# One product of each Winograd layer computed by seven products of quarters, with sums left running in PSUM

## The chip, the cores and the metric

The kernel runs on one core of one Trainium2 chip. Its time is the device time of one execution, in microseconds (us). Engines are named as in the profile: PE (TensorE matmul), PEld (its weight load), DVE (VectorE), ACT (ScalarE), POOL (GpSimd), SP (SyncE, which here only issues DMAs).

## The reference: what is computed

```python
# threshold attention: q, k, v of 8 batches x 8 heads x 576 rows x 64
scores = q @ k.T / 8
scores = where(scores >= max(scores) - tau, scores, -1e9)
attn   = softmax(scores)                   # per row
x      = (attn @ v) laid out as 4608 rows x 512
# hash routing: each row goes to one of 8 experts
expert = token_ids * 2654435761 % 8
for e in range(8):
    h = relu(x[expert == e] @ w1[e])       # 512 -> 1024
    out[expert == e] = h @ w2[e]           # 1024 -> 512
```

Everything is float32. A float32 matmul appears in the trace as two records of a matmul and two of a weight load.

## The kernel before, in words

The first part, up to about 477 us, is attention; the change does not touch it. Towards its end the routing tables are made, the first two experts' weights are loaded, and the first layer of the first expert is computed piece by piece (`early_h`, `late_h`, L633 to L666). `late_h` takes its last PSUM tiles from two pools in turn: `ps_sc` for fo 2 and 4, `ps_m` for fo 0, 1, 3 and 5.

The second part treats the experts one after the other, ordered by size. An expert has room for 544 (the first), 576 (the next four) or 600 (the last three) rows, which stand in the free dimension, cut in two halves of 272, 288 or 300 (240 in the second layer of the last expert, whose remaining 120 rows are done by `last_tile`). So a layer is out = W^T x with W cut into 2 x 2 blocks a11 to a22 and x into b11 to b22. Both layers use the Winograd form of Strassen's scheme: seven block products instead of eight, on four sums of each operand. `left` and `right` give the sums of the weights and of the inputs:

```python
return [sub(s3, a11, a21), add(s1, a21, a22), sub(s2, s1, a11), sub(s4, a12, s2)]
return [sub(t3, b22, b12), sub(b12, b12, b11), sub(t2, b22, b12), sub(t4, b21, t2)]
```

`seven` runs the products. Layer 1 calls it twice (groups g = 0 and 1, 256 of the 512 columns of a weight block each), each for two column blocks of 128; layer 2 calls it once with twice the inner length. In records: 8 a product in layer 1, 16 in layer 2, 112 a layer in both. A product goes into a PSUM tile of two banks; `bank2` takes them in turn from the pools `ps_sc` and `ps_m`, two tiles in each, four in all. ACT copies the first product out (`p1`), and DVE adds every other product to what is needed: c11 = p1 + a12 b21, u2 = p1 + s2 t2, u3 = u2 + s3 t3, c21 = u3 + a22 t4, u4 = u2 + s1 t1, c22 = u3 + s1 t1, c12 = u4 + s4 b22. In layer 1 ACT then applies Relu in place.

The order of the work around it is written out by hand. `seven` calls `after(step)` at six points, and `side1` and `side2` put there what other engines are to do meanwhile: the sums of the second layer's weights (`w2_work`), of h (`h_work`), of the next expert's weights and inputs (`x_work`), the transposes of the next expert's gathered rows (`turns`: five `squares` on DVE, then `move`, 16 DMAs on SP's queue that fill `xT`), the output transposes `put_squares(e, 0)` and `(e, 1)` on DVE, followed by some nine or ten row scatters each on POOL's queue, the row gathers `fetch(e + 2)` on POOL's queue, and the weight loads on SP's queue. Each engine works through its own list in this order and waits where data or a buffer is not there.

The second-layer weights of all experts but the last are read "dealt": the columns of one 128-wide stationary operand are every fourth word of the tile (every second word of the sums' tile).

Of the kernel before, what the change touches and what calls it, by code (L numbers as in the profile page):

```python
# [9 lines left out]
FP32 = mybir.dt.float32  # L10
# [10 lines left out]
def kernel(  # L21
# [17 lines left out]
    P = 128  # L39
# [787 lines left out]
    with tc.tile_pool(name="m_x", bufs=1) as m_x, \  # L827
         tc.tile_pool(name="m_o", bufs=3) as m_o, \
# [9 lines left out]
        o_end = m_x.tile([P, DIN], FP32, name="o_end")  # L838
# [4 lines left out]
        w2_s = m_s.tile([P, 3, FH, D2], FP32, name="w2_s")  # L843
        h_s = m_s.tile([P, 3, FH, CH], FP32, name="h_s")
        halves = [m_s.tile([P, 2, CH], FP32, name=n) for n in ("p1", "u2", "u3", "u4")]
# [3 lines left out]
        turn = [0]  # L849

        def bank2():
            turn[0] ^= 1
            if turn[0]:
                return ps_sc.tile([P, 2, 512], FP32, name="sc")
            return ps_m.tile([P, 2, 512], FP32, name="bank2")
# [31 lines left out]
        def w2_sums(e):  # L887
            t = triple(w2_s, 0, FH)
            return t if e == E - 1 else [dealt(x, C2) for x in t]
# [19 lines left out]
        def sums_w2(e):  # L909
            s1 = None  # L910
            if e == E - 1:
                spare = w_pool.tile([P, CO, F], FP32, name="w1_sb")
                s1 = w_tiles["s1"] = spare[:, :, 0:D2]
            return left(*w2_blocks(e, w_tiles[e, 2]), w2_sums(e), s1)
# [11 lines left out]
        def seven(a, a_s, b, b_s, m0, outs, relu, after):  # L926

            (a11, a12, s1, a22), (s2, s3, s4) = a, a_s
            (b11, t1, b21, b22), (t2, t3, t4) = b, b_s
            c11, c12, c21, c22 = outs  # L930
            n_k, width, dealt_out = a11.shape[1], b11.shape[2], len(a11.shape) == 4
            p1, u2, u3, u4 = (t[:, :, 0:width] for t in halves)

            def product(x, y):
                ps = bank2()
                for i in range(2):
                    c0 = m0 + P * i
                    for c in range(n_k):
                        lhsT = (x[:, c, :, i] if dealt_out else
                                x[:, c, c0:c0 + P])  # L940
                        nc.tensor.matmul(ps[:, i, 0:width], lhsT=lhsT, rhs=y[:, c],  # L941
                                         start=c == 0, stop=c == n_k - 1)
                return ps[:, :, 0:width]

            def out(c, ps, u, step):
                add(c, ps, u)()
                if relu:
# [249 lines left out]
```

## Time and profile before

| | |
|---|---|
| three runs, us | 944.19, 938.54, 937.22 (median 938.54) |
| the profiled execution's own time | 931.3 us |
| its span, first to last instruction | 929.7 us |
| granted TensorE clock | 0.996 |
| PE, DVE, ACT, POOL busy, us | 909.8, 757.5, 457.3, 403.7 |
| first record of the first expert's layer 2 | 501.02 us |
| last matmul group begins | 920.41 us |

A row of the order in time gives start and duration in us, engine, line, operation, output and inputs by tile name, shapes and the number of merged records. Names lose their numbers: `bank` is a tile of `ps_m`, `sc` one of `ps_sc`, `w_s` and `w_sb` are weight sums and weights, `h_s` and `x_s` sums of inputs. A matmul's end is modelled and overlaps the next one's start, so the cost of a product is read from start to start. A row of waits tells who waited for whom, in total, how often, and the longest.

### The profile page before, as it was taken

What the parts mean: (1) busy time and instruction counts of PE and PEld (TensorE: products, weight loads), DVE (VectorE), ACT (ScalarE), POOL (GpSimd) and SP (SyncE); (2) the same over time, 40 slices, a digit from 0 to 9 for tenths busy, and PEclk for the clock granted to TensorE, in tenths of its full rate; (3) what the DMA queues carried; (4) which work ended last, traced back from release to release, by engine and by line L of the source; (5) the groups of instructions that cost most, each with busy time, mean ns of one, the idle gap of its engine ahead of it and who ended that gap; (6) DMA issues with size and microseconds to landing.
All of it is one profiled execution on the core that took longest, in us unless ns stands there. A gap on an engine that the chain in (4) does not pass through costs nothing.

```text
span 929.7 us, 20725 instructions
## 1 busy us (share of the span) xinstructions
PE 909.8 (98%) x7495; PEld 662.0 (71%) x7495; DVE 757.5 (81%) x1654; ACT 457.3 (49%) x741; POOL 403.7 (43%) x528
## 2 busy tenths in 40 slices
PE   7999999999999999999999999999999999999996
PEld 4666666656666566665678888788887978878785
DVE  7999999999999999999955776767668676777551
ACT  6888888888888898888812010110201021020110
POOL 4232432456666623455423370724527073440702
PEclk9999999999999999999999999999999999999999
DMA  7354463554545668743101745364372536412101
GB/s 175 92 148 118 109 152 93 136 131 103 123 105 153 159 165 214 216 107 88 30 25 51 237 131 158 133 173 141 95 223 75 164 133 165 157 34 50 48 3 55
DMA packets 114775, 113.11 MB, mean 122 GB/s; under 512 B 32475, under 2 KB 89315, under 8 KB 114672
## 3 DMA queue, kind: packets, MB, share of 16 engines
q1 hardware_dynamic: 105168, 92.64, 37.0%
q0 software_dynamic: 9072, 18.91, 7.0%
q8 instruction: 61, 1.00, 0.4%
q14 instruction: 42, 0.34, 0.1%
q10 hardware_dynamic: 432, 0.21, 0.1%
HBM read 81.99 MB, written 21.44 MB: 111 GB/s over the span
## 4 chain that ended last, share of the span: by engine, by line
PE 65%; issue 21%; POOL 7%; DVE 3%; ACT 2%; DMA 1%; another core or an unknown queue 1%; POOLq 0%; SPq 0%; DVEq 0%; ACTq 0%
PE av L313 18%; PE sc L235 15%; PE tr L282 11%; PE sc L941 9%; PE bank L941 8%; POOL out_dram L1036 6%; PE sc L640 2%; PE av L282 1%; POOL xg L119 1%; ACT w L260 1%; DVE ns L246 1%; DVE w L271 1%; ACT wT_b L303 1%; ACT wT_a L303 0%
## 5 line engine op out<-in xcount | busy, mean ns | idle before, releaser
L260 ACT ACTIVATE w<-ns,nmx 128x576 f32<-128x576 f32 x288 | 220.5, 777 | 28.8 <-DVE ns L246 27.8
L271 DVE SCALAR_TENSOR_TENSOR w<-ns,thr,w 128x576 f32<-128x576 f32 x288 | 225.8, 816 | 0.0
L1036 POOL DMA_INDIRECT out_dram<-o_q,qidx x127 | 138.1, 1087 | 191.7 <-DVE o_q L1028 153.1
L246 DVE TENSOR_SCALAR_CACHE_REDUCE ns<-sc 128x576 f32<-128x576 f32 x288 | 205.6, 747 | 8.1 <-PE sc L235 7.4
L253 POOL TENSOR_SCALAR thr<-nmx,drop 128x2 f32<-128x2 f32 (+1 forms) x160 | 104.4, 653 | 187.3 <-DVE ns L246 177.6
L235 PE MATMUL sc<-k_sb,q 64*128 64x288 f32 (+1 forms) x1280 | 179.2, 423 | 1.0 <-DVE drop L704 0.7
L282 PEld LDWEIGHTS tr<-ident,w 64*128 64x128 f32 x2624 | 106.0, 138 | 95.4 <-ACT wT_b L303 32.4
L282 PE MATMUL tr<-ident,w 64*128 64x64 f32 x2624 | 139.5, 231 | 6.0 <-ACT wT_b L303 2.6
L948 ACT ACTIVATE h<-h 128x576 f32<-128x576 f32 (+1 forms) x56 | 38.7, 693 | 164.8 <-DVE h L861 126.1
L235 PEld LDWEIGHTS sc<-k_sb,q 64*128 64x128 f32 (+1 forms) x1280 | 93.0, 177 | 23.2 <-DVE ns L246 9.4
L313 PE MATMUL av<-wT_a,v 128*64 128x320 f32 (+1 forms) x704 | 100.6, 418 | 0.2
L303 ACT COPY wT_a<-tr 128x512 f32<-128x512 f32 (+1 forms) x128 | 81.7, 638 | 20.7 <-PE tr L282 20.2
L303 ACT COPY wT_b<-tr 128x512 f32<-128x512 f32 (+1 forms) x128 | 81.4, 636 | 17.1 <-PE tr L282 11.2
L313 PE MATMUL av<-wT_b,v 128*64 128x256 f32 x640 | 83.2, 389 | 0.0
L313 PEld LDWEIGHTS av<-wT_a,v 128*64 128x64 f32 x704 | 43.8, 137 | 29.3 <-DVE xm L352 0.7
L951 ACT COPY p<-bank 128x576 f32<-128x576 f32 (+2 forms) x11 | 7.0, 633 | 99.5 <-PE bank L941 72.5
L313 PEld LDWEIGHTS av<-wT_b,v 128*64 128x64 f32 x640 | 40.2, 136 | 18.8 <-issue 0.7
L542 POOL DMA_INDIRECT slot_scratch<-tok,slot_i x36 | 45.0, 1251 | 9.4 <-issue 7.6
L941 PE MATMUL bank<-h,w_sb 128*128 128x288 f32 (+3 forms) x192 | 48.1, 404 | 0.0
L941 PE MATMUL sc<-h,w_sb 128*128 128x288 f32 (+3 forms) x192 | 47.7, 401 | 0.0
L941 PEld LDWEIGHTS bank<-h,w_sb 128*128 128x128 f32 x192 | 46.6, 300 | 0.5
L941 PEld LDWEIGHTS sc<-h,w_sb 128*128 128x128 f32 x192 | 45.9, 289 | 0.6
(197 smaller groups left out, 1303.7 us busy)
## 6 DMA issues: line engine op xcount, KB each, us to landing
w_sb<-in_moe_w_dram SPq DMA_DIRECT2D x16, 2048.0 KB
q<-in_q_dram SPq DMA_DIRECT2D x62, 288.0 KB
v<-in_v_dram SPq DMA_DIRECT2D x32, 256.0 KB
x_scratch<-xm SPq DMA_DIRECT2D x32, 256.0 KB
xT<-xq SPq DMA_DIRECT2D x84, 80.0 KB
k_sb<-in_k_dram SPq DMA_DIRECT2D x31, 144.0 KB
k_sb<-in_k_dram SPq DMA_DIRECT2D x32, 112.0 KB
x_scratch<-xg SPq DMA_DIRECT2D x9, 256.0 KB
```

The lines of the kernel that those rows point to most:

```text
L235: nc.tensor.matmul(sc[out_rows, i, 0:S2], lhsT=q_sb[rows, h, q0:q1], rhs=k_sb[rows, h], start=True, stop=True)
L246: nc.vector.tensor_scalar(out=ns[:].rearrange("p (i s) -> p i s", i=2), in0=sc[:, :, 0:S2], scalar1=-1.0, scalar2=None, op0=ALU.mult, op1= ...
L253: nc.gpsimd.tensor_scalar(out=thr[:, 0:j + 1], in0=stats[n][0][:, 0:j + 1], scalar1=drop[:], scalar2=None, op0=ALU.add)
L260: nc.scalar.activation(w, nss[n, j][:], AF.Exp, bias=stats[n][0][:, j:j + 1], scale=-1.0)
L271: nc.vector.scalar_tensor_tensor(out=w, in0=nss.pop((n, j))[:], scalar=stats[n][1][:, j:j + 1], in1=w, op0=ALU.is_le, op1=ALU.mult, accum_ ...
L282: nc.tensor.transpose(dst[:, r, 64 * c:64 * c + 64], src[rows, c0:c0 + P], ident[rows, rows])
L303: nc.scalar.copy(dst, tr[:, :, 0:64 * n_c].rearrange("p r (c q) -> p r c q", c=n_c))
L313: nc.tensor.matmul(av[64 * j:64 * j + 64, g, c0:c1], lhsT=v_sb[:, c, 64 * j:64 * j + 64], rhs=wT[g][:, i, c0:c1], start=(c == 0), stop=stop)
L542: nc.gpsimd.indirect_dma_start(out=slot_dram[c % 2][:, :], out_offset=bass.IndirectOffsetOnAxis(ap=slot_i[:, c:c + 1], axis=0), in_=tok[:, ...
L941: nc.tensor.matmul(ps[:, i, 0:width], lhsT=lhsT, rhs=y[:, c], start=c == 0, stop=c == n_k - 1)
L948: nc.scalar.activation(c, c, AF.Relu)
L1036: inst = nc.gpsimd.indirect_dma_start(out=rows[:, :], out_offset=bass.IndirectOffsetOnAxis(ap=idx, axis=0), in_=o_sb, in_offset=None, boun ...
```

## The change

Three things are changed in the experts' part.

First, one of the seven products of each layer of experts 1 to 7, a12 b21, is itself computed by seven products of its quarters (class `Quarters`), again in Winograd's form. In layer 1 it covers both groups at once: its four results are written to c11's place in h, and each group's p1 is added to them there. Its operand sums are new: four of the weights (`inner_w`, into `wi_s`) and four of the inputs (`inner_b`, into `bi_s`), each a quarter of a block. For layer 2 of experts 1 to 6, ACT first copies the block a12 into contiguous quarters (`copy_quarters`, into `w2_q`). The sum s4 is then written over a12 (over a spare tile for the last expert), and `w2_s` shrinks to two blocks.

Second, sums run on in PSUM. u2 is formed by adding s2 t2 onto p1's bank, u3 by adding s3 t3 onto u2's, c21 by adding a22 t4 onto u3's; c12 is s4 b22 added onto s1 t1. ACT copies a bank out at each stage that is needed later (`p1`, `u2`, `mid`), and Relu of c21 reads PSUM. DVE is left with the sums for c11, c12 and c22. Four fixed tiles (`banks`) take the place of the alternation.

Third, expert 0's second layer, which keeps a whole a12 b21, begins in `banks[3]`, uses `banks[2]` and `banks[0]`, and has its products in another order (first, a12 b21, s2 t2, s1 t1, s3 t3, s4 b22, a22 t4). The side work is dealt out anew over eleven points in layer 1 and five in layer 2. The pool `m_o` and `o_end` go; `xg_bufs` take their place in the last outputs.

```diff
-        w2_s = m_s.tile([P, 3, FH, D2], FP32, name="w2_s")
+        w2_s = m_s.tile([P, 2, FH, D2], FP32, name="w2_s")
+        w2_q = m_s.tile([P, 4, 2, P], FP32, name="w2_q")
...
+        def late_tile(fo):
+            if fo in (2, 4):
                 return ps_sc.tile([P, 2, 512], FP32, name="sc")
             return ps_m.tile([P, 2, 512], FP32, name="bank2")
...
+        def products(ps, x, y, start, mid=None):
+            for i, lhsTs in enumerate(x):
+                for c, lhsT in enumerate(lhsTs):
+                    nc.tensor.matmul(ps[:, i], lhsT=lhsT, rhs=y[:, c], start=start and c == 0,
+                                     stop=c == len(lhsTs) - 1, skip_group_check=not start)
+                if i == 0 and mid:
+                    mid()
...
+        class Seven:
...
+            def first(self):
+                products(self.x, self.a[0], self.b[0], True)
+            def keep_p1(self):
+                nc.scalar.copy(self.p1, self.x)
+            def second(self, y):
+                y = y[:, :, 0:self.x.shape[2]]
+                products(y, self.a[1], self.b[2], True)
+                self.out(self.outs[0], y, self.p1)
+            def u2_sum(self):
+                products(self.x, self.a[4], self.b[4], False)
+                nc.scalar.copy(self.u2, self.x)
+            def s1_t1(self, keep):
+                products(self.z, self.a[2], self.b[1], True)
+                if keep:
+                    nc.scalar.copy(self.mid, self.z)
+            def u3_sum(self, keep):
+                products(self.x, self.a[5], self.b[5], False)
+                if keep:
+                    nc.scalar.copy(self.mid, self.x)
+            def c21(self):
+                products(self.x, self.a[3], self.b[6], False)
...
+            def c12(self, mid=None):
+                products(self.z, self.a[6], self.b[3], False, mid)
+                self.out(self.outs[1], self.z, self.u2)
...
+        class Quarters:
...
+            def p1_p2(self):
+                products(self.x, self.a[0], self.b[0], True)
+                nc.scalar.copy(self.p1, self.x)
+                products(self.y, self.a[1], self.b[2], True)
+            def c11(self):
+                add(self.outs[0], self.y, self.p1)()
+            def p5_u2(self):
+                products(self.z, self.a[2], self.b[1], True)
+                nc.scalar.copy(self.p5, self.z)
+                products(self.x, self.a[4], self.b[4], False)
+                nc.scalar.copy(self.u2, self.x)
+            def c12_c22(self):
+                products(self.z, self.a[6], self.b[3], False)
+                add(self.outs[1], self.z, self.u2)()
+                products(self.x, self.a[5], self.b[5], False)
+                add(self.outs[3], self.x, self.p5)()
+            def c21(self):
+                products(self.x, self.a[3], self.b[6], False)
+                nc.scalar.copy(self.outs[2], self.x)
...
         def layer1(e, side):
...
+            q = quarters_of(e, 1, *banks[1:])
+            g0, g1 = group(0, banks[0], banks[2]), group(1, banks[1], banks[3])
+            g0.first()
+            g0.keep_p1()
+            side(0)
+            q.p1_p2()
+            q.c11()
+            g0.u2_sum()
+            side(1)
+            q.p5_u2()
+            g0.s1_t1(True)
+            side(2)
+            q.c12_c22()
+            side(3)
+            g0.u3_sum(False)
+            q.c21()
+            g0.c22(g0.x)
+            side(4)
+            g0.c12()
+            g0.c11(g0.p1)
+            g1.first()
+            g0.relus()
+            side(5)
+            g1.c11(g1.x)
+            g1.relus()
+            g0.c21()
...
         def layer2(e, side):
...
+            o = Seven(a, w2_sums(e), h_blocks(0, FH, half), triple(h_s, 0, FH, half), 0, outs,
+                      False, *((banks[0], banks[1]) if e else (banks[3], banks[2])))
+            o.first()
+            o.keep_p1()
+            if e == 0:
+                o.second(banks[0])
+                run(w2_first)
+                side(0)
+                o.u2_sum()
...
+            q = quarters_of(e, 2, *(banks[i][:, 0:1] for i in (2, 3, 3)))
+            q.p1_p2()
+            q.c11()
+            run(inner_b(second_blocks(e, 2)[1]), 4)
+            o.u2_sum()
+            q.p5_u2()
+            side(0)
+            o.u3_sum(True)
...
         with tc.manual_schedule():
-            run(sums_w2(0), 4)
+            w2_first = sums_w2(0)
+            run(w2_first, 3)
...
+                    def side1(step):
+                        if step == 1 and e == 1:
+                            put_squares(0, 0)
+                        if step == (0 if e > 1 else 2):
+                            put_squares(e - 1, 1)
+                        if step == 2 and more:
+                            copy_quarters(e)
+                        run(w2_work, (0, 1, 2, 0, 3, 1, 1, 0, 0, 0, 0)[step])
+                        run(h_work, 2 if step in (8, 9) else 0)
+                        run(turns, (0, 0, 0, 0, 0, 0, 1, 2, 1, 1, 1)[step])
...
+                    run(x_work, ((1, 2, 3, 10, 0) if e else (2, 2, 0, 4, 8))[step])
...
-                    if more and step == 3:
+                    if more and e and step == 4:
                         put_squares(e, 0)
```

## The prediction

> **What bounds the kernel now.** I read the busy table first, then the expert stage alone (from about 501 us to the end): its stretches by layer, PE's own waits, and the order of products in time. All times here are microseconds of the profiled execution unless marked ns.
>
> The busy table of the page:
>
> ```profile
> PE 909.8 (98%) x7495; PEld 662.0 (71%) x7495; DVE 757.5 (81%) x1654; ACT 457.3 (49%) x741; POOL 403.7 (43%) x528
> ```
>
> PE never rests for long. The next view cuts experts 1 to 3 into layers (columns: stretch, its length, busy us of PE, weight loads, DVE, ACT, POOL, then clock and DMA share):
>
> ```profile
> 527.00:554.10 27.10, 27.10 (x113) 21.28 (x112) 24.37 (x31) 5.27 (x8) 20.08 (x19) 1.00 0.50 183
> 554.10:583.30 29.20, 27.58 (x114) 24.91 (x114) 19.17 (x22) 1.90 (x3) 5.91 (x7) 1.00 0.61 171
> 583.30:610.50 27.20, 27.20 (x114) 21.37 (x113) 20.65 (x26) 5.28 (x8) 20.72 (x20) 1.00 0.36 123
> 610.50:637.60 27.10, 27.10 (x113) 24.84 (x113) 19.45 (x23) 1.90 (x3) 2.87 (x3) 1.00 0.59 162
> ```
>
> The reader is to see that PE fills a layer from end to end, that DVE is at 70 to 90% of a layer and ACT at under 20%. All the time PE loses to others from 490 us on stands in PE's waits (line waited for: total, times, longest):
>
> ```profile
> PE bank L941 <- DVE h_s L858: 1.9, 2, 1.6
> PE sc L941 <- ACT p L951: 0.6, 1, 0.6
> PE bank L941 <- ACT p L951: 0.5, 1, 0.5
> PE bank L941 <- DVE h L861: 0.2, 1, 0.2
> PE sc L941 <- DVE h L861: 0.2, 1, 0.2
> ```
>
> That is 3.4 us in seven experts. So the stage is a stream of matmuls, and a change is worth what it takes out of that stream, minus the holes it makes. The price of one matmul comes from the order in time (start, duration, group, number of records; a float32 matmul shows as two records, each with its own weight load):
>
> ```profile
> 501.02 3.90 PE L941 MATMUL sc<-h,w_sb 128*128 128x272 f32 x16
> 504.76 3.90 PE L941 MATMUL bank<-h,w_sb 128*128 128x272 f32 x16
> 508.49 3.83 PE L941 MATMUL sc<-h_s,w_s 128*128 128x272 f32 x16
> 512.16 3.83 PE L941 MATMUL bank<-h_s,w_s 128*128 128x272 f32 x16
> ...
> 532.80 2.10 PE L941 MATMUL sc<-x_s,w_s 128*128 128x288 f32 x8
> 534.74 2.10 PE L941 MATMUL bank<-x_s,w_sb 128*128 128x288 f32 x8
> ...
> 920.41 1.91 PE L990 MATMUL sc<-w_sb,h 128*120 128x128 f32 x16
> ```
>
> Starts give the cost. 288 columns: 1.94/8 = 242.5 ns a record; 272 columns: 3.67/16 = 229.4 ns; both are columns x 0.833 ns + 2.5 ns. With weights read from the dealt (every fourth word) second-layer tile the 272 case takes 3.74/16 = 233.8 ns: there the weight load sets the pace, and at 288 it hides. Products of expert 5 to 7 (300 columns) start 2.02 apart: 252.5 ns. The last row, 128 columns against 120 weight columns, is (1.91 - 0.273)/15 = 109 ns a record with its last duration of 273 ns taken off: the same formula, so short matmuls keep the rate.
>
> **What the Trainium skill says.** "TensorE: Matmul & The Clock Gate", Back-to-back issue gap, says that in a stream of weight loads and matmuls both set the spacing, so that short matmuls fall behind the streaming rate; its section on LDWEIGHTS prices a load at columns / 1.2 GHz, an estimate of 107 ns for 128. The trace agrees that a load hides behind 288 columns, and its 109 ns row shows no extra at 128. "PSUM — Partial Sum Buffer", PSUM bank collisions raise a hardware error, says two engines must not touch a bank at once. So a product that adds onto a bank must wait until the copy out of it is done. The trace has such a hand-over: an ACT copy from 826.13 for 0.66, PE at 826.85, 0.06 later. Nothing before shows a PE that writes again onto a bank just read, which is the new thing here.
>
> **The change, part by part.**
>
> *Products.* In each of 14 layers (both of experts 1 to 7) the product a12 b21, 8 matmuls of half width (16 records; in layer 1 over both groups), becomes 14 matmuls of quarter width (28 records). For 288 columns: before 112 x 0.2425 = 27.16; after 96 x 0.2425 + 28 x (144 x 0.833 + 2.5 = 122.5 ns) = 23.28 + 3.43 = 26.71. Gain 0.45, eight layers: 3.6. For 300 columns: 28.28 against 24.24 + 28 x 0.1275 = 27.81; gain 0.47, five layers: 2.35. The last layer (240 columns, 202.5 ns; quarter of 120, taken at the measured 109) gains 22.68 - 19.44 - 3.05 = 0.2. Sum **6.1 us**, all on the path. The unknown is 28 short records with full 128-column weights: from below the formula's 122.5 ns, from above the 190 ns that one contiguous 128-column weight load lasts in the group rows, if loads didn't overlap each other. I take 122.5, because the 109 ns row has loads of 183 ns that do overlap. The dealt weights would cost 234 ns, but the change copies them to w2_q first.
>
> *DVE.* Each big set loses the adds for u2, u3, u4 and c21: 4 x 0.755 (576 elements), three sets an expert, 9.1 us. Added: six quarter adds and sixteen small sums. The slope between 576 elements (755 ns) and 1024 (1219) is 1.04 ns, so 288 costs 0.46, 256 0.42, 144 0.31: 3 x 0.46 + 3 x 0.31 + 8 x 0.42 + 4 x 0.31 + 4 x 0.46 = 8.8. DVE stays where it was, with 10 to 30% free; nothing lands on the path by volume, only by order.
>
> *ACT.* Copies of u2, mid and c21 (0.63 each, 0.69 with Relu replaced), four quarter copies (0.63 less 288 x 0.833 = 0.39) per layer and the weight copy (1024 elements, about 1.05): some 8 us an expert, on an engine with 7 busy of 54. Hidden by volume.
>
> *New waits of PE on ACT.* In each layer a set's first product is copied out and then added onto. ACT starts 0.24 after the product's end (585.23 to 585.47), takes 0.63, and PE resumes 0.06 later: 0.93. Between lie two quarter products, 8 x 122.5 ns = 0.98. Covered by 0.05; at 300 columns 0.96 against 1.02. The same margin stands before u3 in layer 2: three tight places an expert, 21 in all. The other re-used banks have a big product (1.94 or 3.88) in between. If that cover is gone each place costs up to 0.93. I take 0.
>
> *Expert 0's second layer.* It now begins in banks[3], the second of ps_m, whose last tenant is late_h's fo 5. DVE reads that one from 501.22 for 0.72; the first product started at 501.02 in the other pool. It must now wait to 502.0: **+1.0**. s4 moves into the dealt a12: 16 x 4.4 ns = +0.1. DVE's turns of x come behind the second product's add and s4, at about 511.6 instead of 509.4. SP then issues 16 moves of 0.6 us; they landed 12.3 us after the last turn (512.47 to 524.76), now near 527.0, against expert 1's first product near 528.0: hidden by 1 us. But the x sums (4 x 0.76) and the inner sums (4 x 0.31) wait for them until 531.2, and then DVE owes in layer 1 of expert 1: q.c11, put_squares(0,0) 1.9, a w2 sum 1.2, put_squares(0,1) 2.1, two sums 2.4, two quarter adds 0.8; it ends near 540.0. PE wants bank 1 for the quarter's c21 at 538.8: **+1.3**. Later experts have put_squares(e,0) a layer earlier and land with 0.6 us or more to spare, by the same ledger. POOL gets the output scatters a few us later; it is busy 26 of the 56 us of a layer pair (20.08 + 5.91). SP's queue: moves one step later in layer 1, needed 16 us into layer 2, landing about 9 us in.
>
> *What stays.* Four DVE waits of 10.0 us in all, and ACT waits of 1.4 and 2.8, are put down to "remote", no engine or queue of the program. They cause most of the 3.4 us above. The change doesn't touch their cause, so I keep 3.4, with 0 and 7 as ends. The tail after the last matmul (922.3 to the end) has the same steps.
>
> Sum: -6.1 + 1.0 + 0.1 + 1.3 = **-3.7**. The profiled execution took 931.3 (span 929.7 and 1.6 around it); it becomes 927.6. The median shown is 938.54, 7.2 above that execution, and I carry the difference over: **934.8**, 0.4% less.
>
> **Rivals.**
>
> *Slower: the banks' turn-round.* The mechanism: PE adds onto a bank that ACT or DVE has just read, at about eight places an expert (g0's u2, the quarter's c21, g1's u2, u3, c21; in layer 2 u2, u3, the quarter's c21), 56 in all. If queueing of copies and adds behind other work costs 0.3 each, that is 16.8: 938.5 - 3.7 + 16.8 = 951.6. It decides from (9.4 + 3.7)/56 = 0.23 us a place. For it: margins of 0.05 to 0.6 us, and in-order engines. Against: ACT is nearly idle, and DVE's waits are mostly for PE, not PE's for it.
>
> *Slower: weight loads.* At 190 ns the short records cost 392 x 67.5 ns = 26.5: 961. It passes +1% from 122.5 + 13.1/392 = 156 ns. Against: the 109 ns row.
>
> *Faster: the holes close.* If the 3.4 goes too and neither new hole of expert 0 and 1 appears: -9.5, 929.0, just over 1%. For it: four bank pairs instead of two in turn. Against: nothing removes the remote waits.
>
> *The change does not do what it says*: the banks tie products so that PE idles what it saves. That is the turn-round at 0.1 us a place: -3.7 + 5.6, 940.4, no change.
>
> **How the numbers follow.** Forecast 0.62, spread 931 to 939 by the ends of the remote waits and of the tight places; no gain (940.4) 0.07; turn-round 0.15; weight loads 0.06; faster 0.10. The range 929 to 946 leaves out the weight loads, the upper half of the turn-round and the faster end. A measurement of this kernel tells about 1%, 9.4 us, from no change. Faster by over 1%: 0.08 (part of the last case); slower by over 1%: 0.20; within: 0.72.
>
> **What would show it.** Products: 28 records of 144 columns a layer, 122.5 ns apart; layers of 26.7 where they were 27.2. PE's waits: about 1.0 before expert 0's first product, on DVE, and about 1.3 in expert 1 before the quarter's c21; under 0.1 at the copies. DVE busy about equal, ACT up by some 50 us. I am wrong if the short records stand at 150 ns or more, if PE's waits on ACT sum to over 5 us, or if DVE's sums of x come late in later experts.

## The result: 8.8 per cent slower, all of it in layer 1 of experts 1 to 7

The changed kernel takes 1021.88 us (median; 1011.1 to 1025.93), the kernel before, beside it on the same chip, 937.88: a ratio of the means of **1.0877** (95% interval 1.076 to 1.0993; of the medians it is 1.0896). The profiled execution took 1025.6 with a span of 1024.0, against 931.3 and 929.7.

The busy table and the 40 slices (each digit a tenth of a slice; PEclk is TensorE's granted clock) of the page after:

```profile
PE 928.9 (91%) x7663; PEld 680.8 (66%) x7663; DVE 756.0 (74%) x1720; ACT 513.5 (50%) x848; POOL 397.7 (39%) x528
...
PE   8999999999999999999996897985969969879697
...
PEclk9999999999999999999999897997979979979899
```

PE is no longer full from slice 22 on, and from slice 26 on its clock drops in six slices in which it rests or has just rested. The stretches of experts 1 and 2, layer 1 and layer 2 each (stretch, length, busy us of PE, weight loads, DVE, ACT, POOL, then clock, DMA share and GB/s):

```profile
528.10:571.30 43.20, 29.01 (x125) 22.44 (x124) 26.29 (x38) 11.85 (x18) 23.55 (x22) 0.88 0.54 175
571.30:598.40 27.10, 27.10 (x126) 25.43 (x126) 16.80 (x28) 4.12 (x9) 0.00 (x0) 1.00 0.22 78
598.40:639.50 41.10, 31.87 (x126) 24.64 (x125) 21.68 (x30) 11.17 (x17) 23.59 (x23) 0.83 0.39 119
639.50:666.50 27.00, 27.00 (x126) 25.33 (x126) 18.51 (x30) 4.13 (x9) 0.00 (x0) 1.00 0.35 106
```

Layer 2 takes 27.0 (26.7 reckoned); layer 1, 27.2 before, takes 43 and 41 here and 39 to 45 over the seven experts. POOL's column tells what lies beside the long layers and not beside the short ones: the row scatters, 17 or 18 of them, with five gathers of rows. PE's waits from 470 us on (line waited for: total, times, longest), 3.4 us before:

```profile
PE bank L939 <- DVE h L866: 36.0, 8, 10.5
PE bank L939 <- issue: 24.4, 4, 8.5
PE bank L939 <- ACT u L981: 14.3, 1, 14.3
PE bank L939 <- ACT h L1042: 4.2, 2, 2.1
```

Expert 2's layer 1 in order of time shows what such a wait is made of (start, duration, what ran, idle time before it and what ended that); PE's rows first, then DVE's, ACT's, and POOL's first and last scatter:

```profile
606.64 0.65 PE L939 MATMUL bank<-bi_s,wi_s 128*128 128x144 f32 x4
607.13 2.10 PE L939 MATMUL sc<-x_s,w_s 128*128 128x288 f32 x8
611.57 1.21 PE L939 MATMUL bank<-bi_s,w_sb 128*128 128x144 f32 x4 [2.33 <-DVE h L866]
612.57 3.38 PE L939 MATMUL sc<-xT,w_s 128*128 128x288 f32 x8
622.85 4.21 PE L939 MATMUL bank<-xT,w_sb 128*128 128x288 f32 x8 [6.90 <-issue]
...
611.06 0.46 DVE L866 TENSOR_TENSOR h<-bank,q_p 128x288 f32<-128x288 f32 x1 [3.06 <-remote]
617.54 0.76 DVE L866 TENSOR_TENSOR h<-sc,u 128x576 f32<-128x576 f32 x1 [6.03 <-PE sc L939]
...
622.39 0.40 ACT L1042 COPY h<-bank 128x288 f32<-128x288 f32 x1 [13.45 <-remote]
...
599.58 1.01 POOL L1244 DMA_INDIRECT out_dram<-o_q,qidx  x1 [35.60 <-DVE o_q L1236]
...
621.88 0.98 POOL L1244 DMA_INDIRECT out_dram<-o_q,qidx  x1 [0.31 <-issue]
```

The quarter's c22 product ends at 607.29 and DVE, idle, takes it at 611.06, 3.8 us later. PE has waited for that, writes c21 onto the bank until 612.78, and ACT, idle for 13.45, copies it at 622.39: **9.6 us after PE had finished**. PE wanted that bank back (622.85). The large product that ends at 609.23 is read by DVE at 617.54, 8.3 late; PE has begun its next two products by then, at 611.57 and 612.57. The trace's records of the semaphore that PE raises move at 611.03, 617.45 and 622.37, just ahead of these three starts, so the consumer is prompt and the news of PE's end is late. This is called a late delivery from here on. In experts 1 to 7 of this trace deliveries are late only under POOL's stream of scatters, the gathers right behind it and for a few us after.

PE waits 15 times. Ten of the waits, 53.0 us, stand before a product that adds onto a bank which an engine has yet to read. The other five, 25.8 us, stand before the first product of group 1, as at 622.85: it starts a new sum, on the bank in which the quarters' c21 ended one product before.

### The profile page after: what moved, and what is told of

The parts are those of the page before. It is cut to its first block, busy times and chain, and to the rows that moved or that the text cites. A ratio compares the mean times of both kernels' runs of the same rounds, so it can differ in the third digit from the quotient of the medians.

```text
span 1024.0 us, 21305 instructions
## 1 busy us (share of the span) xinstructions
PE 928.9 (91%) x7663; PEld 680.8 (66%) x7663; DVE 756.0 (74%) x1720; ACT 513.5 (50%) x848; POOL 397.7 (39%) x528
## 4 chain that ended last, share of the span: by engine, by line
PE 67%; issue 17%; DVE 6%; POOL 4%; another core or an unknown queue 4%; ACT 2%; DMA 0%; POOLq 0%; SPq 0%; DVEq 0%; ACTq 0%
PE av L313 16%; PE sc L235 13%; PE sc L939 13%; PE bank L939 11%; PE tr L282 10%; POOL out_dram L1244 3%; PE sc L640 2%; PE av L282 1%; DVE ns L246 1%; DVE h L866 1%; DVE w L271 1%; ACT wT_b L303 1%; ACT w L260 1%; DVE xq L1264 1%
## 5 line engine op out<-in xcount | busy, mean ns | idle before, releaser
L260 ACT ACTIVATE w<-ns,nmx 128x576 f32<-128x576 f32 x288 | 220.4, 777 | 30.0 <-DVE ns L246 29.6
L1244 POOL DMA_INDIRECT out_dram<-o_q,qidx x127 | 131.3, 1034 | 267.9 <-DVE o_q L1236 229.5
L939 PE MATMUL bank<-xT,w_sb 128*128 128x288 f32 (+3 forms) x168 | 47.8, 428 | 25.8 <-issue 21.7
L963 ACT ACTIVATE h<-h 128x576 f32<-128x576 f32 (+1 forms) x42 | 28.9, 692 | 75.6 <-DVE h L866 69.4
L939 PE MATMUL bank<-x_s,w_s 128*128 128x288 f32 (+1 forms) x112 | 36.1, 474 | 32.1 <-DVE h L866 17.8
L939 PE MATMUL bank<-h,w_sb 128*128 128x288 f32 (+4 forms) x248 | 62.0, 402 | 0.0
L939 PEld LDWEIGHTS bank<-xT,w_sb 128*128 128x128 f32 x168 | 34.6, 220 | 38.5 <-issue 26.0
L939 PEld LDWEIGHTS bank<-h,w_sb 128*128 128x128 f32 x248 | 58.7, 290 | 0.5
L939 PE MATMUL sc<-h_s,w_s 128*128 128x288 f32 (+2 forms) x224 | 56.6, 406 | 0.0
L313 PEld LDWEIGHTS av<-wT_b,v 128*64 128x64 f32 x640 | 40.2, 136 | 18.8 <-issue 0.7
```

What stands on the lines that cost most here:

```text
L260: nc.scalar.activation(w, nss[n, j][:], AF.Exp, bias=stats[n][0][:, j:j + 1], scale=-1.0)
L313: nc.tensor.matmul(av[64 * j:64 * j + 64, g, c0:c1], lhsT=v_sb[:, c, 64 * j:64 * j + 64], rhs=wT[g][:, i, c0:c1], start=(c == 0), stop=stop)
L939: nc.tensor.matmul(ps[:, i], lhsT=lhsT, rhs=y[:, c], start=start and c == 0, stop=c == len(lhsTs) - 1, skip_group_check=not start)
L963: self.later.append(lambda: nc.scalar.activation(c, c, AF.Relu))
L1244: inst = nc.gpsimd.indirect_dma_start(out=rows[:, :], out_offset=bass.IndirectOffsetOnAxis(ap=idx, axis=0), in_=o_sb, in_offset=None, boun ...
```

## The experiments

Eighteen runs come in six groups; each group had one chip, and the kernel before ran on it too. The chips turned out to differ: deliveries are late on some and on others not at all. The time of the kernel before alone tells which. The edits are shown abridged.

| group | kernel before, us | late deliveries |
|---|---|---|
| the result above | 937.9 | yes |
| 1 | 918.5 | none |
| 2 | 930.7 | yes |
| 3 and 5 (same chip) | 929.2, 936.2 | yes |
| 4 | 918.7 | none |
| 6 | 919.0 | none |

### Group 1: four suspects, on a chip where nothing is late

**a_whole_product**: a12 b21 whole again, all else as after the change.

```diff
-            q.p1_p2(); q.c11()      # and p5_u2, c12_c22, c21; the same in layer 2
+            g0.second(banks[1])
-            w2_work += inner_w(...); copy_quarters(e)
```

> From the changed kernel: a12 b21 is computed whole again in both layers (16 long matmuls instead of 28 short records), so the quarter products, their copies and sums are gone; the running sums in PSUM, the four banks and the place of the scatters stay. The changed kernel is at 1025.6 in its profile, the kernel before at 937.9. If the rows' scatters delay TensorE's semaphores because TensorE issues short matmuls at twice the rate (theory 1), the late deliveries go: 935 to 945, TensorE's waits in layer 1 below 8 us in all. If the running sums, with the consumer waiting for a bank that TensorE wants back, are what turns lateness into loss (theory 2), little changes: 1005 to 1030. If the place of the scatters within layer 1 is the cause (theory 3), also 1005 to 1030.

**b_no_scatter**: put_squares without its scatters.

```diff
-            for s in range(s0, s1):
+            for s in range(0):
                 put_rows(o_q[i][:, s - s0] ...
```

> From the changed kernel: the scatters of the finished rows of experts 0 to 6 are left out (their turns on VectorE stay), so those rows are not written; nothing else differs. If the scatters on GpSimd are what TensorE's semaphores are late for (theories 1 and 3), DVE's and ACT's waits of 5 to 15 us in layer 1 go and the time is 922 to 935, near the 934.8 forecast less what the last scatters cost. If the late deliveries come from TensorE's own stream of short matmuls and running sums and the scatters merely lie beside them (theory 4), the time stays at 1005 to 1030.

**c_short_in_before**: in the kernel before, layer 1's a12 b21 in half-width matmuls.

```diff
+                if relu and x is a12:
+                    for i in range(2):
+                        for k in range(2):
+                            for c in range(n_k):
+                                matmul(ps[:, i, w*k:w*k+w], x[:, c, c0:c0+P], y[:, c, w*k:w*k+w])
```

> From the kernel before: in layer 1 each matmul of a12 b21 is issued as two of half the width (32 more records of 144 columns and as many fewer of 288 per expert and group pair); banks, sums, order, scatters as before. If short records during the scatters make the semaphores late (theory 1), the time goes up by tens of us: 970 to 1025, with DVE waits on late TensorE semaphores over 5 us. If it takes the running sums (theory 2) or the scatters' place (theory 3), it stays at 937 to 950; the additional records alone cost at most 32 x 2.5 ns per expert, and their weight loads up to 2 us per expert.

**d_scatter_in_layer2**: the scatters of expert e-1 behind a GpSimd copy that reads expert e's last h.

```diff
         def side2(step):
             if step == 0:
+                nc.gpsimd.tensor_copy(mark[0:1, :], h_0[0:1, 6, 0:1])
+                put_all(e - 1, 0); put_all(e - 1, 1)
```

> From the changed kernel: the scatters of expert e-1 are held on GpSimd until the last h of expert e's layer 1 is written, and so run beside layer 2 of expert e, where the changed kernel shows no loss; all of them are still written. If what counts is that they lie in layer 1 with its tight hand-overs (theory 3), 928 to 945. If a stream of short matmuls or running sums under the scatters is enough wherever it is (theories 1 and 2; layer 2 has 56 short records and two running sums too), the loss moves with them: 990 to 1030 with the late deliveries in layer 2. If the scatters are not the cause (theory 4), 1005 to 1030 with the losses still in layer 1.

Measured, one run each, in the order above: 920.1, 922.35, 918.57 and 916.8, the kernel before 918.53. (In a_whole_product the turns of layer 2's output came ahead of its block c21, so the rows written are of an older block; the same work is done.) None shows a late delivery, and so none tells the theories apart. Beside the groups that follow, they show that the chip has a part in it, which no theory had.

### Group 2: the changed kernel itself, and two suspects, on a chip with late deliveries

**after_again** is the changed kernel; **d_again** is d_scatter_in_layer2; **a_whole_again** is a_whole_product with layer 2's c12 moved behind c21.

> The changed kernel itself, unaltered, because on the chip that took the first four experiments neither the kernel before (918.5) nor any of the four showed a late semaphore. If the late deliveries come with the program (any of theories 1 to 3), this run loses here too: 60 to 90 us over the kernel before, with waits of DVE and ACT of 5 to 15 us in layer 1 under the scatters. If they come with the chip (theory 5: the scatters' writes or TensorE's semaphores are slower on some chips, and the change only multiplies what is there), then on a chip where the kernel before shows none this is 915 to 930, within 1 per cent of the kernel before or faster, as the blind sum had it (minus 3.7 us on the profiled run).

> The changed kernel with the scatters of expert e-1 held until the last h of expert e's layer 1 is written. On a chip with late semaphores: 930 to 945 if the place in layer 1 is what counts (theory 3), 990 to 1030 if they follow the scatters into layer 2 (theories 1 and 2). On a chip without them: within 0.5 per cent of the changed kernel and 1 to 4 us below the kernel before (916.8 against 918.5 in the first look).

> From the changed kernel: a12 b21 whole in both layers again, running sums, four banks and place of scatters kept (as in the first run of this kind, with the last product of layer 2 ordered so that its turns come after all of the output). On a chip with late semaphores: 935 to 950 if short records at twice the rate are the cause (theory 1), 1005 to 1030 if running sums or the place of the scatters are (theories 2 and 3). On a chip without: 918 to 921, that is some 4 us above the changed kernel, for the products that it doesn't save.

| run | us | ratio (95%) | layer 1 of experts 1 to 7 | layer 2 of experts 1 to 7 |
|---|---|---|---|---|
| after_again | 998.8 | 1.0755 (1.072 to 1.079) | 38.9 39.1 26.7 39.0 38.0 37.8 29.1 | 27.0 27.0 36.2 27.0 28.1 28.1 23.4 |
| d_again | 1000.4 | 1.0754 (1.0728 to 1.078) | 28.1 32.4 33.7 29.6 35.9 27.8 27.8 | 28.9 30.3 37.3 27.5 45.7 40.2 35.9 |
| a_whole_again | 989.0 | 1.0634 (1.0573 to 1.0694) | 27.2 40.6 28.7 34.6 34.8 37.9 38.4 | 36.5 28.2 32.1 28.2 29.4 29.4 24.4 |

(A layer's length runs from its first matmul to the next layer's.) after_again and d_again came as expected; a_whole_again's 989.0 lies in neither of its two ranges. It keeps 58 of the 68 us with no quarter product in it. Some 7 of the 58 are of its own making (its layer 2 takes 28.2 and 29.4 where nothing is late, 27.2 and 28.3 in the kernel before); the rest shows that short records, and the tight places that the quarters make, are not needed for the loss. d_again keeps all of it: the loss moves to layer 2 with the scatters, and to the layer after. The stretches of its experts 4 to 6, layer 2, layer 1, layer 2, layer 1:

```profile
747.50:775.00 27.50, 27.26 (x126) 25.39 (x125) 18.53 (x30) 4.13 (x9) 20.57 (x20) 1.00 0.47 148
775.00:810.90 35.90, 30.72 (x126) 23.40 (x125) 22.38 (x30) 11.65 (x17) 4.97 (x5) 0.90 0.34 106
810.90:856.60 45.70, 30.46 (x125) 27.00 (x125) 19.44 (x30) 4.35 (x9) 23.59 (x24) 0.85 0.38 117
856.60:884.40 27.80, 27.80 (x125) 21.85 (x124) 21.59 (x30) 11.53 (x17) 0.00 (x0) 1.00 0.29 91
```

The layer with no POOL work is clean (27.8); the first shows that it is not a law: beside 20 scatters and gathers it loses 0.5, and the layer after it pays 8. What both kernels share and the kernel before has not is the running sum, where a product waits until the last one has been copied out of its own bank. (They share the four fixed banks and the new order of the side work too.) after_again also shows that the layer which pays can change from run to run: its expert 3 loses nothing in layer 1 and 9.2 in layer 2.

### Group 3: the scatters, the lead, and layer 1 undone

Theory 6, formed here: in the kernel before a product goes to one of four banks in turn, so that PE can be three products ahead of the reader it needs; a running sum has no such lead.

> From the changed kernel: the scatters of the finished rows of experts 0 to 6 left out again (their rows are not written), on another chip. So far the late deliveries have shown on chips where the kernel before runs at 930 to 938 and not where it runs at 918.5. Where they show: if they need the scatters, this is 918 to 926 and TensorE has under 3 us of waits in layers 1 and 2; if the running sums alone are enough on such a chip (theory 2 in its plain form), it stays above 980. On a chip without them: 920 to 924, which tells nothing new.

928.62 beside 929.19, 2.6 over the range expected, with PE's waits as small as expected. PE's waits from 470 us on and two of the layers:

```profile
PE bank L939 <- DVE h L866: 1.0, 1, 1.0
```

```profile
553.30:580.30 27.00, 27.00 (x125) 25.37 (x125) 18.63 (x30) 4.13 (x9) 0.00 (x0) 1.00 0.37 112
580.30:607.10 26.80, 26.80 (x126) 21.77 (x125) 21.44 (x30) 11.27 (x17) 5.51 (x5) 1.00 0.44 134
```

On a chip with late deliveries, with running sums and quarters, all of the loss is gone once the scatters are; the five gathers that remain beside a layer do no harm alone. (Its time flatters the change less than the layers do: from the last scatter to the end of the span it takes 12.7 us where c_short_again takes 5.7; the trace does not say why.)

**g_two_banks_before**, from the kernel before:

```diff
         def bank2():
-            turn[0] ^= 1
-            if turn[0]:
+            if False:
                 return ps_sc.tile([P, 2, 512], FP32, name="sc")
             return ps_m.tile([P, 2, 512], FP32, name="bank2")
```

> From the kernel before: the seven products of each group take turns on two banks instead of four, so TensorE can be at most one product ahead of the engine that empties them; no running sums, no quarters, same scatters. If what the change took away is TensorE's lead over late semaphores (theory 6: in the kernel before a product goes to a fresh bank three products before that bank is wanted again, so a delivery up to 10 us late costs nothing), this loses on a chip with late deliveries, 960 to 1010, with TensorE waiting on DVE in the layers under the scatters, and no more than 5 us on a chip without them. If the running sums do something of their own (theory 2), it stays within 10 us of the kernel before on either chip.

952.43, 23 us over the kernel before: below what theory 6 named, above what theory 2 did. Some 17 of it is layer 1 at 29.6 in place of 27.2 also in layers where nothing is late, DVE simply being behind; single waits of PE reach 2.9 only, and the longest wait of VectorE that is put down to "remote" is 2.5. In experts 1, 2, 4 and 5, beside 17 or 18 scatters each, DVE takes the last product of layer 1 within 0.08 us of its end: hardly a delivery is late in this run. **Inconclusive**: a shorter lead costs something by itself, but what it makes of late deliveries can't be read from a run that has so few.

> From the kernel before: a12 b21 of layer 1 as half-width matmuls again, on another chip. On a chip with late deliveries: over 960 if short records make them (theory 1), within 6 us of the kernel before if they do not (theories 2, 3, 6). On a chip without: 918 to 919 as in the first look.

929.74 beside 929.19: short records alone do nothing here either. This run, with the kernel before's banks, is the best measure of the lead, for the same program ran in group 1. The end of expert 1's layer 1 there, PE's last product and DVE's reading of it:

```profile
544.57 2.10 PE L942 MATMUL sc<-xT,w_s 128*128 128x288 f32 x8
...
546.71 0.76 DVE L861 TENSOR_TENSOR h<-sc,u 128x576 f32<-128x576 f32 x1
```

and here:

```profile
551.04 2.10 PE L942 MATMUL sc<-xT,w_s 128*128 128x288 f32 x8
...
563.65 3.19 PE L942 MATMUL bank<-h_s,w_s 128*128 128x288 f32 x12 [1.78 <-DVE h_s L858]
...
559.74 0.76 DVE L861 TENSOR_TENSOR h<-sc,u 128x576 f32<-128x576 f32 x1 [4.51 <-remote]
```

Read 0.04 us after its end there, 6.6 us here, and PE, working on, loses 1.8. So **the banks of the kernel before meet late deliveries too**, of two thirds of the 9.6 us above, and hide most of them. (In the profile of the kernel before, DVE stands idle for 4.50 at the same place, also put down to "remote".)

**e_mixed**: layer 1 as before (`seven`, four banks in turn), layer 2 as changed, all scatters from the end of layer 2 on.

```diff
         def layer1(e, side):
-            q = quarters_of(e, 1, *banks[1:])
-            ...                       # the running sums
+            for g in range(NG):
+                seven(w1_blocks(w), triple(w1_s, 0, C2), x_blocks(e), ..., lambda step: side(g, step))
```

> Layer 1 as in the kernel before (seven products on four banks in turn, sums in SBUF, a12 b21 whole); layer 2 as in the changed kernel (quarters, running sums); all scatters beside layer 1, as in the changed kernel. If the lead over late deliveries is what counts (theory 6) this is within 5 us of the kernel before on any chip, with its layer 2s at 27.0 us each, about 0.4 us below the kernel before's per expert: 2 to 4 us faster on a chip without late deliveries. If the layer 2 of the change, or scatters that all lie in layer 1, are harmful by themselves (theories 2 and 3), it is 950 to 1000 on a chip with them.

941.29 beside 929.19, 1.0083 (1.0035 to 1.0131), where theory 6 had named at most 5 us over the kernel before. The stretches of expert 1's layer 2 and of expert 3's two layers:

```profile
552.90:592.30 39.40, 29.91 (x126) 26.90 (x126) 21.70 (x29) 5.42 (x11) 9.35 (x10) 0.87 0.42 121
...
646.50:673.60 27.10, 27.10 (x113) 21.27 (x112) 23.14 (x32) 7.24 (x9) 20.02 (x18) 1.00 0.36 120
673.60:700.70 27.10, 27.10 (x126) 25.43 (x126) 17.96 (x24) 4.84 (x10) 6.24 (x6) 1.00 0.61 169
```

Eighteen scatters beside a layer 1 with four banks in turn: no loss. But nothing is late there that the banks could hide. PE's last product of expert 3's layer 1, and DVE's reading of it:

```profile
671.70 2.10 PE L1110 MATMUL bank<-xT,w_s 128*128 128x288 f32 x8
...
673.84 0.76 DVE L866 TENSOR_TENSOR h<-bank,u 128x576 f32<-128x576 f32 x1
```

That is 0.04 us after the product's end, and in the layer 1s of experts 2 to 5 DVE reads at the same distances from PE's ends as on a chip without late deliveries (e2_mixed_earlier below). So the same chip and as many scatters don't always bring them; this run does not tell why.

Expert 1 is the other case. Expert 0's scatters start late, the last four of them and five gathers lie beside expert 1's layer 2, and 12.4 us are lost there, as much as the whole kernel is over the kernel before. PE's longest wait in it is for a bank of layer 1, not for a running sum:

```profile
549.00 2.10 PE L1110 MATMUL sc<-xT,w_sb 128*128 128x288 f32 x8
...
564.48 1.33 PE L939 MATMUL sc<-h,w_q 128*128 128x144 f32 x4 [7.56 <-DVE u L866]
...
563.00 0.76 DVE L866 TENSOR_TENSOR u<-sc,u 128x576 f32<-128x576 f32 x1 [5.19 <-remote]
```

The product that ends at 551.10 is read at 563.00, 11.9 late, and PE wants its bank back at 556.92, 5.8 after that end. So four banks in turn hide some 5.8 us there, and a delivery that is later costs what it is over.

### Groups 4 and 6: no late deliveries again

**e2_mixed_earlier** turns and scatters expert 0's rows ahead of expert 1's layer 1; **r_split_scatter** is the changed kernel with the second half of each expert's scatters held to layer 2; **i_half_scatter** leaves that half out; **h_before_no_scatter** leaves all out of the kernel before (the edit of b).

```diff
 # e2, from e_mixed
+                    if e == 1:
+                        put_squares(0, 0); put_squares(0, 1)
                     layer1(e, side1)
 # r, from the changed kernel; put_squares(e, 1) turns only
                     if step == 0:
+                        nc.gpsimd.tensor_copy(mark[0:1, :], h_0[0:1, 6, 0:1])
+                        put_all(e - 1, 1)
 # i, from the changed kernel, in put_squares
-            for s in range(s0, s1):
+            for s in range(s0, s1 if i == 0 else s0):
```

> The mixed kernel (layer 1 as in the kernel before, layer 2 as in the changed kernel), with both halves of expert 0's rows turned and scattered before expert 1's layer 1 begins on VectorE instead of within it, so that no scatter is left when expert 1's layer 2 begins. In the mixed kernel 12.4 of its 12.1 us over the kernel before were lost in that one layer 2 (39.4 us against 27.0 in the others). If loss comes from running sums that lie beside scatters (theory 6), that layer 2 goes to 27 to 28 us and the kernel to within 3 us of the kernel before, where deliveries are late, and 2 to 3 us below it, where they are not. If layer 2 of expert 1 loses for another reason, it stays within 5 us of 39.

> From the changed kernel: the first half of each expert's scatters stays at the start of layer 1, the second half is held until the last h of that layer 1 is written and so lies at the start of layer 2: two streams of 9 in place of one of 18, all rows written. If lateness builds up along a stream (the first late delivery came 7 to 14 us into the streams of the changed kernel), 940 to 965 on a chip with late deliveries. If each scatter does its own harm wherever it lies beside a running sum, 985 to 1015 there. On a chip without: 915 to 925.

> From the changed kernel: the scatters of the second half of the rows of experts 0 to 6 are left out (those rows are not written), the first half stays where it is, 9 scatters of 1.28 us per expert in layer 1. If lateness builds up along a stream, 928 to 945 on a chip with late deliveries; if each scatter does its own harm, about half of the changed kernel's loss stays, 955 to 975. On a chip without: 920 to 924.

> From the kernel before: the scatters of the rows of experts 0 to 6 are left out (not written). If the kernel before absorbs late deliveries by its lead of three products (theory 6), leaving them out gains only what its layers are over 27.2 and 28.3 us in the profile, about 6 us: 921 to 925 where the kernel before is at 929, and nothing where it is at 918.5. If the scatters cost it as much as they cost the changed kernel, it would gain tens of us, which the layers' lengths speak against.

917.28, 915.18, 919.36 and 927.5 beside 918.68. No delivery is late, so what the last three were for they cannot tell. (Two lie outside what was expected for such a chip: i by 0.6, and h, for which no change was expected, by 9.) h gained nothing in its layers, which are 27.2 and 28.3 from expert 2 on; its 9 us more are mostly the longer end that the version without scatters also had. The mixed kernel is faster than the kernel before by 0.14% (ratio 0.9986, 0.9979 to 0.9993), and again in group 6, on another chip without late deliveries: 917.24 beside 918.95 (0.9982, 0.9975 to 0.999).

> The mixed kernel with expert 0's scatters started before expert 1's layer 1. On a chip with late deliveries (kernel before at 929 to 938): within 4 us of the kernel before if loss needs a running sum beside a scatter (theory 6), the layer 2 of expert 1 at 27 to 29 us; if expert 1's layer 2 loses for another reason, 9 to 14 us above the kernel before with that layer 2 at 36 to 40. On a chip without: 0.9986 of the kernel before again, that is 1.0 to 1.8 us below it.

On a chip with late deliveries this version has not been measured.

### Group 5: does the lateness build up along a stream?

> The changed kernel, unaltered. On a chip where the kernel before runs at 918 to 919 with no late semaphores: 914 to 917, that is 2 to 4 us below the kernel before (the forecast's sum was minus 3.7 for a profiled run; the split version gave 915.2 beside 918.7, the version with scatters in layer 2 916.8 beside 918.5), every layer 1 from expert 2 on at 26.7 or 27.8 us. On a chip where the kernel before runs at 929 to 938: 990 to 1026 as measured before.

> The changed kernel with the second half of each expert's scatters held to the start of layer 2. On a chip with late deliveries: 940 to 965 if the lateness builds up along a stream, 985 to 1015 if each scatter beside a running sum does its own harm. On a chip without: 914 to 916, within 0.2 per cent of the changed kernel.

The changed kernel: 1022.1 beside 936.2, 1.0911 (1.0838 to 1.0984). In two streams: **970.7**, 1.0373 (1.0302 to 1.0443): 51 of its 86 us come back, and the forecast for a build-up is missed by 6. The stretches of r_split_again by layer, experts 2, 3 and 6, layer 1 and layer 2 each (POOL's x15 in the layer 2s of experts 2 and 3: the copy onto `mark`, 9 scatters and 5 gathers):

```profile
588.70:617.80 29.10, 27.52 (x126) 21.48 (x125) 21.42 (x30) 11.16 (x17) 8.93 (x9) 1.00 0.32 103
617.80:653.10 35.30, 30.02 (x126) 27.08 (x126) 18.62 (x30) 4.23 (x9) 14.60 (x15) 0.90 0.45 135
653.10:679.80 26.70, 26.70 (x125) 21.71 (x124) 21.54 (x30) 11.20 (x17) 10.37 (x9) 1.00 0.36 114
679.80:714.80 35.00, 29.82 (x126) 26.98 (x126) 18.67 (x30) 4.23 (x9) 14.60 (x15) 0.90 0.44 136
...
842.70:871.50 28.80, 28.08 (x126) 21.80 (x125) 21.95 (x30) 11.49 (x17) 9.20 (x9) 1.00 0.35 109
871.50:901.00 29.50, 28.34 (x126) 26.12 (x126) 19.05 (x30) 4.35 (x9) 10.70 (x11) 1.00 0.19 50
```

Nine scatters (11.6 us) alone beside a layer cost 0 to 2.4 us. Nine with the five gathers right behind (18.2 us) cost 5 to 9. Ten with no gathers, in expert 6's layer 2, cost 1.4. Seventeen to nineteen, in the changed kernel on the same chip, cost 10.2 to 19.8. So in the changed kernel the lateness does build up along an unbroken stream on POOL's queue, over its first 10 us or so, and gathers that follow keep it up, though gathers alone are harmless. A long stream is not enough by itself: e_mixed's expert 3 has 17 scatters and five gathers without a break, 31.6 us, and nothing late. Putting the gathers apart as well was not tried.

## Why the prediction was wrong

**The step that failed is "What stays".** It found DVE's four waits of 10.0 us put down to "remote", no engine or queue of the program, said that "The change doesn't touch their cause", and kept 3.4. The waits were the reader's sight of late deliveries, and the 3.4 was not their size but what PE still felt of them behind its lead. The change made PE want banks back earlier, and late deliveries that had cost little stood on its path: its waits became 78.9 us, and with the clock at 0.83 to 0.88 of full speed the seven layer 1s lie 101.2 us over their undisturbed lengths (28.1, 26.7 and 27.8 in r_split_scatter). The sum closes on the profiled spans: 101.2 lost, 5.3 less that the kernel before lost in its own layers, 1.1 more up to expert 1, 2.7 gained by the change itself: 94.3, which is 1024.0 - 929.7.

**The rival "banks' turn-round" had the place right and the price wrong.** It asked for 0.23 us a place to decide, priced queueing at 0.3, and gave 951.6. Spread over its 56 places the waits are 1.4 each, though a third of them stands before group 1's first product, which it did not count, and they are not made by queueing: ACT had been idle 13.45 us when it copied. The hand-over of 0.24 that the ledger took from the kernel before is true where nothing is late, and 3.8 to 9.6 in expert 2's layer 1. The other row that it took for a hand-over, ACT's copy at 826.13, carries a wait of 1.43 put down to "remote" itself; and PE at 826.85 does write onto the bank just read, which "Nothing before shows" overlooks. The argument against it, that "DVE's waits are mostly for PE", was the symptom. And "four bank pairs instead of two in turn", its reason for a faster end, was a misreading: the kernel before has four in turn too, and the change took the turn away.

**The bound left out**: the remote waits should have been priced with the lead gone. Single ones of up to 4.5 us stood in the trace before; at one of these in each of seven layer 1s the loss is, by estimate, some 30 us, at two 60.

**The ledger itself held where nothing is late.** Short records stand 122.5 ns apart (600.29 to 600.78 for four), as the trace's 109 ns row had suggested. The Trainium skill's "TensorE: Matmul & The Clock Gate", Back-to-back issue gap, lets short matmuls fall behind the streaming rate; at 144 columns none of that shows. Layer 1 falls from 27.2 to 26.7 and from 28.3 to 27.8, by 0.43 and 0.47 (0.45 and 0.47 reckoned); expert 1's quarter c21 waits 1.0 for DVE (1.3 reckoned), its layer is 28.1. Layer 2 gained 0.13 at 288 columns and 0.20 at 300, of 0.45 and 0.47: four of its six large products take 3.91 to 3.99 in place of 3.88, with no wait named. Expert 0's wait of 1.0 did not show. ACT's weight copy took 2.06, not 1.05, hidden. DVE fell by 1.5 us in all (0.3 an expert, some 2 in all, reckoned), ACT rose by 56 (some 50). From the layers, minus 2.7 in place of minus 3.7; and the changed program with its scatters in two streams measures 915.18 beside 918.68, **minus 3.5**, on a chip with no late deliveries. The changed kernel itself was measured only on chips that have them; that it is as fast as r_split_scatter elsewhere is inferred from b, d, r and i, none of which shows a late delivery there.

**What is shown and what is not.** Shown: the loss needs the scatters (b) and a chip with late deliveries; it goes where the scatters go (d) and shrinks when their stream is broken (r); and it comes with the running sums and fixed banks, for the changed kernel, a and d lose up to 20 us in a layer, while layers with four banks in turn (the kernel before, c, e) lose at most 2.6 but for the one case in e.

Argued and not shown is that the lost lead alone makes the difference. The rival is that the change also makes the deliveries later: e's experts 2 to 5 and most of g's layers show none late beside as many scatters, on a chip where the changed kernel, in group 5, had them in all seven experts. No run keeps the lateness and takes only the lead away; g was to do so and met hardly any. PE's own standing could be what makes the next delivery later.

Open too: why a delivery comes late on such a chip at all, whether POOL's issuing of a scatter or the writing of its rows does it, and whether the chip decides or its state at the time (only one chip came twice, late both times). Every time here is of an execution that left records; whether taking them has a part in the lateness can't be told from these runs.

## What to carry to other kernels

A wait that a profile puts down to nothing in the program is to be priced by what hides it, and a change that shortens the distance between a producer and its own buffer can put it on the path: count the products, and the us, between a write and the need to write there again, before and after. Running a sum on in PSUM saves vector work and a bank, but puts a round trip, PE to reader and back, on the path for each term; keep it away from long streams of indirect DMAs, or break these up (51 of 86 us came back). And run a baseline beside every variant: the chip alone moved the kernel before from 918.5 to 937.9, and r_split's ratio to it from 0.996 to 1.037.

## What was not expected of the hardware

On the chips of groups 1, 4 and 6 no semaphore was late in experts 1 to 7 in any kernel; on the others all kernels with scatters had late ones, 918.5 to 919.0 against 929 to 938 for the kernel before. Not all of that difference is late deliveries under the row scatters: expert 0's layer 2, ahead of any of them, begins at 492.9 to 494.3 us there and at 498.5 to 502.1 here. Why stays open. A second sign is the completion of the scatters. In the DMA part of c_short_in_before, on a chip without late deliveries, they have a time to landing (last column, us):

```profile
out_dram<-o_q,qidx POOLq DMA_INDIRECT x127, 2.7
```

and in that of the changed kernel, where deliveries are late, too few of their completions are recorded to give one (so in all ten traces with row scatters from such chips, while the seven from the others give 2.5 to 3.2):

```profile
out_dram<-o_q,qidx POOLq DMA_INDIRECT x127
```

And PE pays for waiting twice: in the disturbed layers shown its granted clock falls to 0.83 to 0.90 on average, and a product of eight records that lasts 2.10 us takes 4.21 after a wait of 6.90. A wait of 2.33 was enough once: the four records at 611.57 take 1.21 in place of 0.65.
